# Batch 1's attention in four visits instead of six, and the first two w_in groups of batches 1 and 2 interleaved

## The chip, the cores and the metric

One core of one Trainium2 chip. The metric is the device time of one execution in microseconds (us).

## The reference, cut to what matters

```python
batch, n_heads, seq, head_dim = (8, 8, 1024, 64);  k_proj = 64
k_proj = np.einsum('ks,bhsd->bhkd', E, k)
v_proj = np.einsum('ks,bhsd->bhkd', F, v)
scores = scale * np.matmul(q, k_proj.transpose(0, 1, 3, 2))
attn = softmax(scores)                       # cut: max, exp, sum
attn_out = np.matmul(attn, v_proj)
x = attn_out.transpose(0, 2, 1, 3).reshape(8192, 512)
h = x @ w_in                                 # 512 -> 2048
g = h * np.clip(h + 3.0, 0.0, 6.0) / 6.0
return g @ w_out                             # 2048 -> 512
```

The two large products dominate. Attention is small, so the kernel hides it among them.

## The kernel before: the parts that the change and the argument touch

A batch has two blocks (t = 0, 1) of 512 tokens. A block has 16 `first_group`s (w_in, four matmuls each, one for each pair of heads in x, then ScalarE and VectorE make g) and four `second_group`s (w_out, 16 matmuls each). While they run, the attention of the next batch is computed in *visits*: TensorE leaves the w_out group for a round of small matmuls, 64 rows and columns each, four at a time in the array, and comes back. The program uses PSUM as two rings of four banks, `pmm` and `pat`.

Batch 1's attention has a plan of its own. It is spread over block 1 of batch 0, one `next(ahead)` for each four w_out matmuls:

```python
PLAN = ((0, "project"), (0, "keys_out"), (1, "turn"), (0, "values_out", 0), (2, "values_out", 1),
        (1, "two_scores", 0), (2, "two_scores", 2), (2, "normalised", 0),
        (0, "normalised", 1), (0, "normalised", 2), (0, "normalised", 3))
```

That makes six visits: two of `two_scores` (four banks of pat), four of `normalised` (two banks of sums, two of values). The later batches use larger visits, six banks each, of which the last one matters here:

```python
def visit(self, n, following, later):
    ...                                       # n = 0, 1, 2
    early = self.values(2, pmm, pmm)
    den, av = self.sums(3, pmm, pat), self.values(3, pat, pat)
    if following:
        following.project()                   # k and v of the batch after
    self.scaled(2, early, self.recs)          # VectorE: x of pair 2, both blocks
    recs = self.inverses(den)                 # ScalarE: Ln, Ln, Exp, Exp
    if following:
        following.keys_out()                  # VectorE: two copies of the keys
        later += [following.turn] + [lambda a=a: following.values_out(a) for a in range(2)]
    return lambda: self.scaled(3, av, recs)   # VectorE: x of pair 3, called next
```

For batch 2 this last visit is also the last thing before batch 2's own first block, which needs that x. In the later batches there is a whole block between.

The softmax here doesn't subtract the row's maximum and nothing guards it: scores larger than these inputs give would overflow.

## Time and profile before

| | before |
|---|---|
| median, lowest, highest of three runs | 511.65, 511.52, 511.9 us |
| span of the profiled run | 510.0 us |
| TensorE busy | 497.4 us, 98% |
| longest wait of TensorE after the first 48 us | 1.2 us, for x, at batch 2's start |

The prediction below shows the lines and reads them. In a line of a profile, PE is TensorE, PEld its weight loads, DVE VectorE, ACT ScalarE, POOL GpSimd and SPq the queue that issues DMAs. `at` and `mm` are banks of `pat` and `pmm`, `kp` and `kT` keys, `vp` values, `rec` the inverses of the sums, `o_sb` rows of the output. A bracket at the end of a timeline row gives the engine's idle time before the row, and what ended it.

### The profile page before, as it was taken

Reading aid. Unit: us, or ns where it says so; the run is one execution under the profiler, and the core shown is the slowest. Engines: PE = TensorE matmul, PEld = TensorE weight load, DVE = VectorE, ACT = ScalarE, POOL = GpSimd, SP = SyncE. Lnnn points to the kernel's source line nnn. Section 1 sums busy time; section 2 is a strip of 40 time slices with the busy share of each in tenths; the row PEclk is TensorE's granted clock in tenths of the full one; section 3 lists DMA queues with packets and bytes.
Section 4 is the critical chain, followed back from the end, with each engine's and each line's share of the span. In section 5 each row is a group of like instructions: output and inputs, shape, how many; then the busy total and the mean of one; then the engine's idle time right before and its main releaser. Section 6 shows DMA issues by size and latency. Waiting matters only on the chain.

```text
span 510.0 us, 7106 instructions
## 1 busy us (share of the span) xinstructions
PE 497.4 (98%) x2750; PEld 224.3 (44%) x2802; DVE 257.5 (50%) x401; ACT 274.5 (54%) x493; POOL 37.9 (7%) x57
## 2 busy tenths in 40 slices
PE   8899999999899999999999999999999999999996
PEld 3444444444344444444444444444444444444442
DVE  3572735855655733656434743467444563334420
ACT  3657476567576545664466644674447654444431
POOL 8610020010100200002000020000000000000000
PEclk9999999999999999999999999999999999999999
DMA  9999999599299493516924188421110111101112
GB/s 165 199 205 207 202 156 236 97 159 176 88 184 186 91 218 76 125 41 91 225 57 94 52 141 169 107 58 33 42 41 25 38 42 42 42 21 42 41 51 74
DMA packets 74210, 55.39 MB, mean 109 GB/s; under 512 B 35520, under 2 KB 65984, under 8 KB 74176
## 3 DMA queue, kind: packets, MB, share of 16 engines
q0 software_dynamic: 31952, 29.36, 37.0%
q1 hardware_dynamic: 42000, 25.17, 19.4%
q10 hardware_dynamic: 224, 0.39, 0.3%
q8 instruction: 22, 0.36, 0.3%
q14 instruction: 12, 0.10, 0.1%
HBM read 59.24 MB, written 16.78 MB: 149 GB/s over the span
## 4 chain that ended last, share of the span: by engine, by line
PE 94%; DMA 3%; issue 1%; POOL 1%; DVE 0%; ACT 0%; DVEq 0%; POOLq 0%
PE mm L470 43%; PE mm L450 43%; PE at L181 3%; DMA w_in_sb<-in_moe_w_in_dram 2%; PE at L227 1%; PE mm L227 1%; DMA k<-in_k_dram 1%; PE at L209 1%; PE mm L209 0%; PE at L370 0%; POOL q L97 0%; DVE kp L187 0%; POOL k L101 0%; PE at L350 0%; DVE xT L246 0%
## 5 line engine op out<-in xcount | busy, mean ns | idle before, releaser
L456 DVE SCALAR_TENSOR_TENSOR g<-r,mm 128x512 bf16<-128x512 f32 x256 | 173.8, 686 | 131.8 <-ACT r L455 130.4
L470 PE MATMUL mm<-w_out_sb,g 128*128 128x512 bf16 x995 | 231.8, 379 | 1.7 <-issue 0.5
L450 PE MATMUL mm<-xT,w_in_sb 128*128 128x512 bf16 x1001 | 229.2, 379 | 3.1 <-DVE xT L246 1.2
L455 ACT ACTIVATE r<-mm 128x512 f32<-128x512 f32 x256 | 152.8, 599 | 76.2 <-PE mm L450 73.7
L450 PEld LDWEIGHTS <-w_in_sb 128*128 128x128 bf16 x1024 | 99.4, 98 | 124.0 <-issue 5.5
L470 PEld LDWEIGHTS <-g 128*128 128x128 bf16 x1024 | 98.0, 98 | 121.5 <-issue 7.2
L484 ACT COPY o_sb<-mm 128x512 f32<-128x512 f32 x35 | 20.3, 587 | 91.5 <-PE mm L470 91.5
L484 DVE COPY o_sb<-mm 128x512 f32<-128x512 f32 x28 | 19.3, 691 | 67.3 <-PE mm L470 64.2
L159 ACT ACTIVATE rec<-mm 128x512 f32<-128x512 f32 x34 | 19.0, 595 | 34.1 <-PE mm L227 17.6
L163 ACT ACTIVATE rec<-rec 128x512 f32<-128x512 f32 x60 | 35.6, 637 | 0.0
L246 DVE TENSOR_TENSOR xT<-at,rec 128x512 bf16<-128x512 f32 x44 | 28.1, 680 | 7.1 <-ACT rec L163 7.1
L218 ACT ACTIVATE aT<-at 128x512 bf16<-128x512 f32 x44 | 23.1, 613 | 0.9 <-PE at L209 0.9
L159 ACT ACTIVATE rec<-at 128x512 f32<-128x512 f32 x30 | 17.3, 598 | 6.0 <-PE at L227 3.7
L199 POOL COPY mark<-kT 1x1 bf16<-1x1 bf16 x5 | 0.9, 178 | 210.1 <-DMA kT<-kp 210.1
L181 PE MATMUL at<-k,e_t 128*64 128x512 bf16 x56 | 13.4, 382 | 0.0
L181 PE MATMUL at<-v,f_t 128*64 128x512 bf16 x56 | 13.4, 382 | 0.0
L187 DVE CAST kp<-at 64x512 bf16<-64x512 f32 x14 | 9.0, 678 | 4.9 <-PE at L181 4.9
L218 ACT ACTIVATE aT<-mm 128x512 bf16<-128x512 f32 x12 | 6.5, 594 | 8.9 <-PE mm L209 8.9
L190 DVE CAST vp<-at 64x512 bf16<-64x512 f32 x14 | 9.7, 694 | 0.4
L181 PEld LDWEIGHTS <-e_t 128*64 128x64 bf16 x56 | 5.6, 109 | 7.2 <-PE at L227 2.1
L479 DVE COPY o_sb<-mm 128x256 f32<-128x256 f32 x1 | 0.4, 425 | 16.0 <-PE mm L470 16.0
L227 PE MATMUL at<-aT,vp 64*64 64x512 bf16 x88 | 8.5, 376 | 0.0
(62 smaller groups left out, 147.0 us busy)
## 6 DMA issues: line engine op xcount, KB each, us to landing
out_dram<-o_sb SPq DMA_DIRECT2D x63, 256.0 KB, 2.0
k<-in_k_dram POOLq DMA_DIRECT2D x7, 1024.0 KB, 15.4
v<-in_v_dram POOLq DMA_DIRECT2D x7, 1024.0 KB, 21.0
q<-in_q_dram POOLq DMA_DIRECT2D x7, 1024.0 KB, 10.5
w_out_sb<-in_moe_w_out_dram POOLq DMA_DIRECT2D x4, 512.0 KB, 17.1
k<-in_k_dram POOLq DMA_DIRECT2D x4, 256.0 KB, 5.8
v<-in_v_dram POOLq DMA_DIRECT2D x4, 256.0 KB, 7.9
w_in_sb<-in_moe_w_in_dram POOLq DMA_DIRECT2D x2, 512.0 KB, 11.9
```

Of the source, the lines that this page charges most:

```text
L159: nc.scalar.activation(ln, den, AF.Ln)
L163: nc.scalar.activation(ln, ln, AF.Exp, scale=-1.0)
L181: nc.tensor.matmul(ps[e * KP:(e + 1) * KP], ef_t[e][:, so, :], kqv[self.b]["kv"[e]][:, :, so, :], start=(so == 0), stop=(so == SO - 1))
L190: nc.vector.tensor_copy(self.vp[a * KP:(a + 1) * KP], self.ps[KP:].rearrange("p (h d) -> p h d", d=D))
L218: nc.scalar.activation(self.aT[j][:, r].rearrange("p a n -> p (a n)"), tiles[r], AF.Exp, scale=scale)
L227: nc.tensor.matmul(tiles[t][c:c + D].rearrange("p (r n) -> p r n", r=2), stationary(r, 2 * j + a), self.aT[j][r:r + KP, :, a, :], start=Tr ...
L246: nc.vector.tensor_mul(self.xT[:, j, t, :], av[t], recs[t])
L450: nc.tensor.matmul(h_ps, w_in_sb[:, ko, fo * P:(fo + 1) * P], xT[:, ko, t, :], start=(ko == 0), stop=(ko == KO - 1))
L455: nc.scalar.activation(r, h_ps, AF.Relu, bias=0.5, scale=1.0 / 6.0)
L456: nc.vector.scalar_tensor_tensor(g[:, fo, :], r, 1.0, h_ps, op0=ALU.min, op1=ALU.mult)
L470: nc.tensor.matmul(o_ps, g[:, fo, c * P:(c + 1) * P], w_out_sb[:, fo, :], start=(fo == 0), stop=(fo == FO - 1))
L484: (copy or nc.scalar.copy)(o_sb, o_ps)
```

## The change

Its intent: fewer visits, so that TensorE leaves its stream less often; and matmuls that don't need the late pair of x put ahead of the one that waits for it. `PLAN`, `steps`, `two_scores` and `normalised` go. The core of the rest:

```diff
-    for fo in range(2, FO):                      # block 1 of batch 0
-        if fo in (7, 8, 9, 10):
-            next(ahead)
+        pop()
+        if fo == 7:
+            second.project()
+            second.keys_out()
+            later += [second.turn, *(lambda a=a: second.values_out(a) for a in range(2))]
 ...
+    rest = []
     for c in range(SB):
-        for _ in second_group(0, 1, g[1], c, nc.vector.tensor_copy):
-            next(ahead, None)
+        for i, _ in enumerate(second_group(0, 1, g[1], c, nc.vector.tensor_copy)):
+            pop()
+            if i == 0:
+                rest.append(second.visit(c, None, later))
+            elif i == 2 or c == SB - 1:
+                while rest:
+                    rest.pop()()
 ...                                               # main loop, batch b, block t
-                first_group(xT, t, g, fo)
+                if b < 3 and t == 0 and fo < 2:
+                    if fo == 0:
+                        two_groups(xT, t, g, ((0, 1, 2), (3,)))
+                else:
+                    first_group(xT, t, g, fo)
```

`two_groups` with `((0, 1, 2), (3,))` runs pairs 0 to 2 of the first group, pairs 0 to 2 of the second, then pair 3 of each.

More of the change, by code (lines that the diff above doesn't have):

```diff
@@ L281, in visit @@
             return lambda: self.scaled(3, av, recs)
-        def two_scores(self, j):
-            tiles = [self.scores(i, pat) for i in (j, j + 1)]
-            for i in range(2):
-                self.exps(j + i, tiles[i])
-        def normalised(self, j):
-            den, av = self.sums(j, pat, pat), self.values(j, pat, pat)
-            recs = self.inverses(den)
-            yield
-            self.scaled(j, av, recs)
-            yield
-            yield
-        def steps(self, plan):
-            for wait, part, *args in plan:
-                for _ in range(wait):
-                    yield
-                yield from getattr(self, part)(*args) or ()
-    PLAN = ((0, "project"), (0, "keys_out"), (1, "turn"), (0, "values_out", 0), (2, "values_out", 1),
-            (1, "two_scores", 0), (2, "two_scores", 2), (2, "normalised", 0),
-            (0, "normalised", 1), (0, "normalised", 2), (0, "normalised", 3))
     class First:
@@ L503, with two_groups @@
     g = [g_tile(), g_tile()]
-    def two_groups(t, kos, more):
+    def two_groups(xT, t, g, kos, more=lambda: None):
         tiles = [pmm(), pmm()]
@@ L512, in two_groups @@
         for fo in range(2):
-            h_out(tiles[fo], g[t], fo)
-    two_groups(0, ((0, 1), (2,), (3,)), lambda: next(by_pairs, None))
+            h_out(tiles[fo], g, fo)
+    two_groups(xT, 0, g[0], ((0, 1), (2,), (3,)), lambda: next(by_pairs, None))
     for fo in range(2, FO):
@@ L519, with pop @@
             first.queries(1, (0, 1) if fo == FO - 2 else (2, 3))
-    ahead = Attention(1)
-    ahead.xT = x_next
-    ahead = ahead.steps(PLAN)
+    behind, later = [], []
+    second = Attention(1)
+    second.xT = x_next
+    def pop():
+        if later:
+            later.pop(0)()
     rows = [second_group(0, 0, g[0], c) for c in range(SB)]
@@ L530 @@
             first.second_values(2 * i - 2)
-    two_groups(1, ((0, 1), (2, 3)), lambda: None)
+    two_groups(xT, 1, g[1], ((0, 1), (2, 3)))
     for fo in range(2, FO):
         first_group(xT, 1, g[1], fo)
-        if fo in (7, 8, 9, 10):
-            next(ahead)
+        pop()
[3 more added lines that the diff above has]
+            later += [second.turn, *(lambda a=a: second.values_out(a) for a in range(2))]
         elif fo == 11:
             whole(rows[3])
+    rest = []
     for c in range(SB):
-        for _ in second_group(0, 1, g[1], c, nc.vector.tensor_copy):
-            next(ahead, None)
+        for i, _ in enumerate(second_group(0, 1, g[1], c, nc.vector.tensor_copy)):
[5 more added lines that the diff above has]
+                    rest.pop()()
     qT_dma[2] = q_transposed(2)
-    whole(ahead)
     xT = x_next
-    behind, later = [], []
     second = Attention(2)
@@ L558 @@
             for fo in range(FO):
-                first_group(xT, t, g, fo)
-                if later:
-                    later.pop(0)()
+                if b < 3 and t == 0 and fo < 2:
[3 more added lines that the diff above has]
+                    first_group(xT, t, g, fo)
+                pop()
                 if b > 1 and t == 0 and fo == 5 and third:
```

## The prediction

> **What bounds the kernel now.** I read the page first (who is busy), then the waits of TensorE, then the chain, then the timeline of the two places that the change touches.
>
> ```profile
> PE 497.4 (98%) x2750; PEld 224.3 (44%) x2802; DVE 257.5 (50%) x401; ACT 274.5 (54%) x493; POOL 37.9 (7%) x57
> ...
> PE 94%; DMA 3%; issue 1%; POOL 1%; DVE 0%; ACT 0%; DVEq 0%; POOLq 0%
> PE mm L470 43%; PE mm L450 43%; PE at L181 3%; DMA w_in_sb<-in_moe_w_in_dram 2%; PE at L227 1%; PE mm L227 1%; DMA k<-in_k_dram 1%; PE at L209 1%; PE mm L209 0%; PE at L370 0%; POOL q L97 0%; DVE kp L187 0%; POOL k L101 0%; PE at L350 0%; DVE xT L246 0%
> ```
>
> TensorE is busy for 98% of a span of 510.0 us and is 94% of the chain that ends last; no other engine is over 54%. The change adds and removes no matmul, so it can only take away time in which TensorE starts none. The waits of TensorE between 48 and 136 us, the stretch that the change touches, show one real wait:
>
> ```profile
> PE mm L450 <- DVE xT L246: 1.2, 1, 1.2
> ```
>
> The unit for the rest is the spacing of 512-column matmuls. The chain in order of time gives it, as two neighbouring pieces of 16:
>
> ```profile
> 171.94 3.45 PE mm L470 x16
> 175.40 3.45 PE mm L450 x16
> ```
>
> 3.45/16 = 0.216 us from start to start. (The 379 ns of one matmul in the page is pipelined; I don't add those.)
>
> First place: batch 1's attention, which block 1's w_out groups hide. TensorE's timeline (start, length, then what):
>
> ```profile
> 70.58 0.63 PE L209 MATMUL at<-qT,kT 64*64 64x256 bf16 x16
> 71.14 1.90 PE L470 MATMUL mm<-w_out_sb,g 128*128 128x512 bf16 x8
> 72.97 0.41 PE L227 MATMUL at<-aT,ones 64*64 64x512 bf16 x4
> ...
> 76.23 0.41 PE L227 MATMUL at<-aT,ones 64*64 64x512 bf16 x4
> 76.47 0.39 PE L227 MATMUL at<-aT,vp 64*64 64x512 bf16 x4
> 76.78 2.76 PE L470 MATMUL mm<-w_out_sb,g 128*128 128x512 bf16 x12
> 79.48 0.41 PE L227 MATMUL at<-aT,ones 64*64 64x512 bf16 x4
> ```
>
> Here are six visits to the attention: two of 16 score matmuls (68.19, 70.58) and four of 4 sums and 4 values (72.97, 76.23, 79.48, 82.73). From the 12 matmuls at 76.78 to the visit at 79.48 pass 2.70 us, where 12 x 0.216 = 2.59: about 0.1 lost on the way in. A visit itself takes 76.78 - 76.23 = 0.56 us to the next w_out matmul, for two rounds of four concurrent tiles, which at 0.216 each would be 0.43: the other 0.1 is the way out. The same kernel already has visits of six banks, in batch 1's own second block:
>
> ```profile
> 114.00 0.41 PE L227 MATMUL mm<-aT,ones 64*64 64x512 bf16 x4
> ...
> 114.24 0.39 PE L227 MATMUL at<-aT,vp 64*64 64x512 bf16 x4
> ...
> 114.45 0.39 PE L209 MATMUL at<-qT,kT 64*64 64x256 bf16 x8
> ...
> 114.77 1.41 PEld L470 LDWEIGHTS <-g 128*128 128x128 bf16 x8 [0.20 <-issue]
> ```
>
> Three rounds of four in 114.77 - 114.00 = 0.77 us.
>
> Second place: the start of batch 2's first block, where the one wait lies.
>
> ```profile
> 133.92 0.82 PE L450 MATMUL mm<-xT,w_in_sb 128*128 128x512 bf16 x2
> 134.05 1.28 DVE L187 CAST kp<-at 64x512 bf16<-64x512 f32 x2 [0.76 <-PE at L181]
> 135.26 1.27 DVE L246 TENSOR_TENSOR xT<-at,rec 128x512 bf16<-128x512 f32 x2
> 135.98 2.97 PE L450 MATMUL mm<-xT,w_in_sb 128*128 128x512 bf16 x13 [1.25 <-DVE xT L246]
> ```
>
> The first w_in group runs its pairs 0 to 2 (one of the three records is missing), then its fourth matmul waits for pair 3 of x, which VectorE writes only after two copies of the next batch's keys. The fourth could have started about 134.58 (133.92, 0.01 of switching, 3 x 0.216); it starts at 135.98: 1.40 us lost.
>
> **What the Trainium skill says.** "TensorEngine Tiling (Array Packing)", Key Properties: "Changing tiling mode (not just tile) drains the TensorE". The trace agrees: about 0.1 us each way. "TensorE: Matmul & The Clock Gate", Wait — 56ns, not 53.3ns?, gives 215.7 ns from start to start for 512 columns at full clock; the trace has 216. The same page, Architectural detail, says that ScalarE and VectorE queues are strict first in, first out; so x behind the key copies is what the DVE lines above show. "Perfetto Trace Analysis", Matmuls, asks that independent groups rotate through different PSUM banks so that evacuation overlaps; that is the condition that the larger visits must meet.
>
> **The change part by part.**
>
> (a) Six visits become four of six banks. Removed: six ways in of 0.10 and six visits of 0.56 us, 0.60 + 3.36 = 3.96. Added: four ways in of 0.10 and four visits of 0.77, 0.40 + 3.08 = 3.48. Saved: 0.48 us, all on TensorE's own stream, so all on the path, if no visit has to wait. Finer sums of the single starts give 0.46.
>
> The visits now come after the first four matmuls of each of four w_out groups, so every 16 x 0.216 + 0.10 + 0.77 = 4.33 us, against 7.8 us where the kernel has such visits already. Who must keep up? Visit 0 starts where the first score visit did, 68.19; queries and keys landed before 67.06 (the GpSimd copy that waits for them). Visit 1, at 72.52, needs exponentials: ScalarE takes six at 0.52 from 68.64, done 71.8, the pair needed by sums at 70.7. Visit 2, at 76.85, needs the banks of pair 0's values: in the old visit at 72.97 the second product ends at 76.34, 3.37 later, so now at 75.9. Visit 3, at 81.18, needs the inverses of pair 2: ScalarE after visit 2 has four Ln at 0.54 and four Exp at 0.58, 4.5 us from 77.3, done 81.8; only VectorE waits for the last of them. It multiplies pair 2 until about 83.1, and pair 3 (Ln and Exp after visit 3, first done about 83.5) until 84.9. Batch 1's first block then starts at about 84.56 instead of 85.03, and needs pair 3 half a microsecond or more later: no wait. The banks: in the compiled program of the kernel before, 384 of 392 tiles of the ring of four take the bank that was released longest ago in program order. By that order no visit takes the bank of the w_out group just ended, except visit 3's denominators, which take the bank of the group that ended 1.4 us before; its copy needs 0.43 + 0.69 = 1.12 us.
>
> (b) Batch 2's first two groups: three matmuls of the second group go ahead of the wait. The wait's end is set by VectorE (keys, then x), which this does not move against the visit. So 3 x 0.216 = 0.65 us of the 1.40 is filled, and 0.75 stays. After it both groups end within 0.43 us, and VectorE falls behind: products at about 137.0 and 137.7, a value copy, the third product until about 139.9. The next visit would come at 139.96 (140.61 less 0.65) and wants that bank: it just fits, or loses 0.1.
>
> (c) The same at batch 1's start saves nothing: the chain shows no wait there before, and by (a) none after. Value copies one group later, no more and no fewer instructions elsewhere.
>
> Sum: -0.46 - 0.65 = -1.11 us; 511.65 - 1.11 = 510.54. With a tenth lost to the tight places I say 510.6, a gain of 0.2%.
>
> **The rivals.** First: bank waits in the closer visits. If the first w_in group of batch 1 or a visit's tile gets the bank of a w_out group that has just ended, TensorE stands 1.12 - 0.22 = 0.9 us each time (copy latency less one spacing), and (a) turns to a loss: 511.5 with one, 514 with four. For it: visits 4.33 us apart and VectorE copies behind products in one queue. Against: the order of release above. Second: ScalarE or VectorE becomes the bound in this stretch: ScalarE was busy 12.9 of the 17.8 us from 67.2 to 85.0, the same work now fits in 17.3, 75%; for it, the work bunches; against it, nothing is needed sooner than a visit later. It would cost some tenths: 511.0. Third: the filled 0.65 us is given back at batch 2's next visit, whose banks and keys (landed by 138.15) then bind: 511.2. Fourth: the filled wait is worth nothing because x comes later; I see no reason in the DVE order.
>
> **Range and chances.** The three runs before lie within 0.4 us. All rivals but four-fold bank waits stay between 510.4 and 511.7. I give 510.2 to 511.4. A 2% change would need 10 us, ten times what TensorE idles in these places.
>
> **What would show it right or wrong.** Right: four visits of about 0.77 us in block 1, 4.33 us apart; batch 1's first w_in matmul near 84.6; the wait for x at batch 2 present still, at about 0.6 in the list of waits instead of 1.2, with six w_in matmuls ahead of it; later pieces of the chain all shifted by about 1.1 us. Wrong: a new wait of TensorE on an o_sb copy, on rec or on g in 68 to 90 us, or on g at batch 2's first visit; or x of pair 3 later than 2.05 us after the first w_in matmul of batch 2.

## The result, and the profile after

Six runs: 510.52 us median (510.4 to 510.6), against 511.5 us (511.27 to 511.9) for six runs of before: 0.98 us less. The ratio of the two is 0.998, 95% interval 0.9967 to 0.9993. It is a small gain, clear of the noise, and "the same" by a 2% measure.

(Line numbers differ between the profiles, since the change removes lines: w_in is L450 before and L424 after, w_out L470 and L444.) The page has TensorE as busy as before in a shorter span (508.7 us):

```profile
PE 497.5 (98%) x2750; PEld 224.3 (44%) x2802; DVE 258.0 (51%) x401; ACT 274.0 (54%) x493; POOL 37.9 (7%) x57
```

TensorE's timeline in block 1 (start, length, line, what):

```profile
68.11 0.61 PE L209 MATMUL at<-qT,kT 64*64 64x256 bf16 x16
68.65 3.63 PE L444 MATMUL mm<-w_out_sb,g 128*128 128x512 bf16 x16
72.21 0.41 PE L227 MATMUL mm<-aT,ones 64*64 64x512 bf16 x4
...
76.54 0.41 PE L227 MATMUL mm<-aT,ones 64*64 64x512 bf16 x4
76.78 0.39 PE L227 MATMUL at<-aT,vp 64*64 64x512 bf16 x4
77.00 0.39 PE L227 MATMUL at<-aT,ones 64*64 64x512 bf16 x4
77.31 3.63 PE L444 MATMUL mm<-w_out_sb,g 128*128 128x512 bf16 x16
80.87 0.41 PE L227 MATMUL mm<-aT,vp 64*64 64x512 bf16 x4
```

Visits start 4.33 us apart (72.21, 76.54, 80.87), and the one at 76.54 takes 77.31 - 76.54 = 0.77 us. No row of the whole stretch has a wait for a bank.

The start of batch 2's first block, all engines:

```profile
133.14 1.47 PE L424 MATMUL mm<-xT,w_in_sb 128*128 128x512 bf16 x5
133.28 1.28 DVE L187 CAST kp<-at 64x512 bf16<-64x512 f32 x2 [0.76 <-PE at L181]
134.48 1.27 DVE L246 TENSOR_TENSOR xT<-at,rec 128x512 bf16<-128x512 f32 x2
...
135.21 2.32 PE L424 MATMUL mm<-xT,w_in_sb 128*128 128x512 bf16 x10 [0.60 <-DVE xT L246]
...
139.01 0.69 DVE L190 CAST vp<-at 64x512 bf16<-64x512 f32 x1
...
139.43 0.74 PE L209 MATMUL at<-qT,kT 64*64 64x256 bf16 x16
```

Six matmuls run before the wait (five recorded; a few per cent of the records are missing), where three ran before. The wait, marked 1.25 before, is 0.60 now. And something new: the last rounds of scores of batch 2's first visit take 0.74. The same row of the kernel before has 0.61:

```profile
140.85 0.61 PE L209 MATMUL at<-qT,kT 64*64 64x256 bf16 x16
```

To place the difference I took single starts of TensorE from both traces and cut the run into stretches. The wait in this table is the distance between the two w_in starts less one spacing of 0.216, so a little more than the profile's own figure.

| stretch (us) | before | after | difference |
|---|---|---|---|
| start to the key projection of batch 1 | 55.009 | 54.689 | -0.320 |
| from there to batch 1's first w_in matmul (block 1) | 30.017 | 29.556 | -0.461 |
| from there to batch 2's first w_in matmul | 48.891 | 48.893 | +0.002 |
| from there to the end of batch 2's first visit | 7.471 | 6.964 | -0.507 |
| of it: the wait for x | 1.408 | 0.764 | -0.644 |
| of it: the visit | 0.782 | 0.919 | +0.137 |
| from there to the end | 368.647 | 368.646 | -0.001 |

The stretches are from one profile of each kernel. The two that the change touches give -0.461 - 0.507 = -0.968 us, and the medians say -0.98. The -0.320 of the first stretch is no part of it: nothing is changed there, and over the twelve profiles that stretch lasts 54.39 to 55.01 us, with the profile of before at the top.

### The profile page after: what moved, and what is told of

Read it like the earlier page. It is cut to its first block, busy times and chain, and to the rows that moved or that the text cites. A ratio compares the mean times of both kernels' runs of the same rounds, so it can differ in the third digit from the quotient of the medians. Undisturbed runs are those within 1.5% of the kernel's fastest.

```text
span 508.7 us, 7106 instructions
## 1 busy us (share of the span) xinstructions
PE 497.5 (98%) x2750; PEld 224.3 (44%) x2802; DVE 258.0 (51%) x401; ACT 274.0 (54%) x493; POOL 37.9 (7%) x57
## 4 chain that ended last, share of the span: by engine, by line
PE 94%; DMA 2%; POOL 2%; issue 1%; DVE 0%; ACT 0%; DVEq 0%; POOLq 0%
PE mm L444 44%; PE mm L424 43%; PE at L181 3%; DMA v<-in_v_dram 2%; PE mm L227 2%; PE at L227 1%; PE at L209 1%; POOL q L97 1%; PE mm L209 1%; POOL k L101 1%; POOL v L101 0%; PE at L344 0%; DVE kp L187 0%; PE at L324 0%; PE at L312 0%
## 5 line engine op out<-in xcount | busy, mean ns | idle before, releaser
L444 PE MATMUL mm<-w_out_sb,g 128*128 128x512 bf16 x997 | 231.6, 379 | 1.8 <-issue 0.6
L424 PE MATMUL mm<-xT,w_in_sb 128*128 128x512 bf16 x999 | 229.1, 379 | 1.8 <-DVE xT L246 0.6
L424 PEld LDWEIGHTS <-w_in_sb 128*128 128x128 bf16 x1024 | 99.4, 98 | 122.8 <-issue 4.8
L444 PEld LDWEIGHTS <-g 128*128 128x128 bf16 x1024 | 98.1, 98 | 121.6 <-issue 7.0
L159 ACT ACTIVATE rec<-mm 128x512 f32<-128x512 f32 x39 | 21.8, 595 | 37.0 <-PE mm L227 20.1
L246 DVE TENSOR_TENSOR xT<-at,rec 128x512 bf16<-128x512 f32 x42 | 26.9, 680 | 5.1 <-ACT rec L163 5.1
L159 ACT ACTIVATE rec<-at 128x512 f32<-128x512 f32 x25 | 14.6, 599 | 2.3 <-PE at L344 2.3
L218 ACT ACTIVATE aT<-mm 128x512 bf16<-128x512 f32 x14 | 7.6, 594 | 9.5 <-PE mm L209 9.5
L246 DVE TENSOR_TENSOR xT<-mm,rec 128x512 bf16<-128x512 f32 x14 | 9.0, 682 | 0.6 <-PE mm L227 0.6
L84 PE MATMUL mm<-ones 128*128 128x512 bf16 x18 | 7.4, 548 | 1.5 <-DVE ones L77 1.5
```

The costliest lines, as they stand in the source:

```text
L159: nc.scalar.activation(ln, den, AF.Ln)
L218: nc.scalar.activation(self.aT[j][:, r].rearrange("p a n -> p (a n)"), tiles[r], AF.Exp, scale=scale)
L246: nc.vector.tensor_mul(self.xT[:, j, t, :], av[t], recs[t])
L424: nc.tensor.matmul(h_ps, w_in_sb[:, ko, fo * P:(fo + 1) * P], xT[:, ko, t, :], start=(ko == 0), stop=(ko == KO - 1))
L444: nc.tensor.matmul(o_ps, g[:, fo, c * P:(c + 1) * P], w_out_sb[:, fo, :], start=(fo == 0), stop=(fo == FO - 1))
```

## The experiments

Ten runs in three calls, the first on chip 9, the others on chip 13. Each is set beside runs of before on its own chip. Differences of some tenths in the medians are near the spread of the runs, since the start varies: by the runs' times alone, visits alone (95% interval of the ratio to before 0.9977 to 1.0002) and five visits (0.9973 to 1.0) are not clear of the noise. The stretches after the start repeat to 5 ns where an edit leaves them alone, the long last one to 0.03 us, so the verdicts rest on them.

| kernel | median (us) | before, same chip | block 1 stretch | wait for x, batch 2 | batch 2's first visit |
|---|---|---|---|---|---|
| visits alone | 511.01 | 511.44 | 29.556 | 1.410 | 0.781 |
| pair alone | 510.90 | 511.44 | 30.018 | 0.762 | 0.919 |
| no pair at batch 1 | 510.70 | 511.44 | 29.556 | 0.763 | 0.918 |
| x first | 509.72 | 511.44 | 29.555 | 0 | 0.919 |
| five visits | 510.72 | 511.38 | 29.787 | 0.763 | 0.919 |
| late visit | 510.26 | 511.38 | 29.556 | 0.763 | 0.782 |
| x first, late visit | 509.60 | 511.38 | 29.556 | 0 | 0.782 |
| after again | 510.42 | 511.46 | 29.556 | 0.762 | 0.918 |
| x first, no pair | 509.53 | 511.46 | 29.556 | 0 | 0.782 |
| value copy on ScalarE | 510.36 | 511.46 | 29.555 | 0.764 | 0.782 |

### One part at a time

`visits_alone` is the changed kernel without the interleaved groups:

```diff
-                if b < 3 and t == 0 and fo < 2: ... two_groups ...   # cut
-                else:
-                    first_group(xT, t, g, fo)
+                first_group(xT, t, g, fo)
```

> Batch 1's attention in four visits, batches 1 and 2 start as before. My theory (a tiling switch costs 0.1 us each way, nothing else in block 1): block 1's w_out stretch is 0.46 us shorter than before, the wait for x at batch 2 is the whole 1.41 us again, no loss in batch 2's first visit; about 0.46 us under before, 0.5 over the changed kernel. Rival (the two parts help each other, or the visits shift later waits): something clearly else than 0.46.

`pair_alone` is the kernel before (six visits) with the interleaved groups at batch 2 only (cut: `two_groups` takes `xT` and `g`, as in the change):

```diff
-                first_group(xT, t, g, fo)
+                if b == 2 and t == 0 and fo < 2:
+                    if fo == 0:
+                        two_groups(xT, t, g, ((0, 1, 2), (3,)))
+                else:
+                    first_group(xT, t, g, fo)
```

> The old six visits, and the paired start only at batch 2. My theory: 0.65 us of the wait filled, 0.14 given back in batch 2's first visit, where the score tiles wait for the bank of the value copy; 0.51 us under before, and the two parts alone add up to the whole 0.97. Rival (the filled time is given back entirely, or the end of the wait moves): 0 to 0.2 under before.

Measured: the visits alone shorten block 1 by 0.461 us and leave the wait at 1.41; the pair alone shortens the wait by 0.646 and lengthens the visit by 0.137, and leaves block 1 as it was. In the medians that is 0.43 and 0.54 us; together 0.97, what the whole change gives. The parts are independent, and the longer visit belongs to the pair.

`no_pair_batch1` keeps all but the interleaving at batch 1 (`b < 3` becomes `b == 2`).

> The changed kernel, but batch 1's first two groups not interleaved. My theory: the x of batch 1 is there before its first group asks for it, so the pair there does nothing: equal to the changed kernel within 0.05 us in the trace. Rival (with visits closer together, pair 3 of batch 1 comes late and the pair hides it): a new wait for x near 85 us, up to 0.65 us slower.

Measured: the stretches of the table as in the changed kernel to 3 ns, no wait at batch 1. The "batch 1" half of that edit does nothing, because its x is there in time either way. (The median is 0.2 us above the changed kernel's, which ran on another chip. Its profile's start is 0.2 us longer, 54.895 us, and the rest agrees to 0.02 us.)

### Is it the number of visits?

`five_visits` cuts visit 1 of block 1 in two, so that its score round comes four w_out matmuls later:

```diff
             if n == 1:
                 den, av = self.sums(0, pmm, pmm), self.values(0, pat, pat)
-                last = self.scores(3, pat)
                 recs = self.inverses(den)
-                self.exps(3, last)
+                if self.b > 1:
+                    self.exps(3, self.scores(3, pat))
 ...
+            elif i == 1 and c == 1:
+                second.exps(3, second.scores(3, pat))
```

> The changed kernel with visit 1 of block 1 cut in two: its eight score matmuls come four w_out matmuls later as a fifth visit. My theory (each visit costs two tiling switches and nothing else): from the first key projection to batch 1's first w_in matmul 29.56 us in the changed kernel, here 29.78 (0.10 in, 0.1 out, 0.01 each of two rounds that start cold); 0.2 us slower in the trace. Rival (the gain came from where visits lie against the banks, not from their number): no difference, or far more than 0.2.

TensorE's timeline of that kernel, around the added visit:

```profile
71.95 0.41 PE L227 MATMUL mm<-aT,ones 64*64 64x512 bf16 x4
72.19 0.39 PE L227 MATMUL at<-aT,vp 64*64 64x512 bf16 x4
72.51 1.04 PE L444 MATMUL mm<-w_out_sb,g 128*128 128x512 bf16 x4
73.48 0.41 PE L209 MATMUL at<-qT,kT 64*64 64x256 bf16 x8
73.82 2.76 PE L444 MATMUL mm<-w_out_sb,g 128*128 128x512 bf16 x12
```

The four w_out matmuls from 72.51 to the visit at 73.48 take 0.97 us where a full stream takes 0.86: the way in, plus 0.01 of a slower first start. The score round takes 73.82 - 73.48 = 0.34 us. The stretch is 29.787 us, 0.231 longer than with four visits. One visit more costs 0.23, two fewer gave 0.461: the price is per visit, and the rival (it is where they lie against the banks) falls.

The loss comes with the change of tile shape, not whenever TensorE turns to another product. In the profile of before, after the first 21.5 us, 30 of 33 starts of a round of 64x64 tiles came 0.309 or 0.310 us after the 128x128 matmul before them. From w_in to w_out, both 128x128, it was 0.215 or 0.216 in 51 of 54. (The others, at 0.525 and 0.43, are one spacing longer: a record is missing.) What fills the 0.093 us stays open. At a change, the weight load starts with its matmul (both at 139.18 in the changed kernel, in batch 2's first visit), where in a stream it starts about 0.2 us ahead (63.56 and 63.78 in the kernel before). So a late weight load and a drained array would look alike here, and no run separates them.

### What sets the end of the wait?

`x_first` splits the product for pair 3. The half that batch 2's first block needs goes ahead of the key copies in VectorE's queue:

```diff
             if following:
+                nc.vector.tensor_mul(self.xT[:, 3, 0, :], av[0], recs[0])
                 following.keys_out()
                 later += [following.turn] + [...]
+                return lambda: nc.vector.tensor_mul(self.xT[:, 3, 1, :], av[1], recs[1])
             return lambda: self.scaled(3, av, recs)
```

> The changed kernel, with VectorE's product for pair 3 of the first half of x ahead of the two key copies (the other half stays behind them). My theory (the wait is set by VectorE's order, not by ScalarE's inverses or by TensorE): the first inverse is done about 0.6 us before the key copies start, so the wait at batch 2 of 0.76 us is gone; key copies start about 0.15 us later and nobody waits for them; 0.76 us under the changed kernel, less if batch 2's first visit then waits longer. Rival (x is late because its inverses are late): at most 0.2 us better.

Measured: the wait is gone, and from batch 2's first w_in matmul to the end of its first visit it is 6.203 us against 6.964, 0.761 less. So x was late only because two copies that nobody waited for yet stood ahead of it.

`x_first_no_pair` is the same without any interleaved groups:

> Four visits, the first half of pair 3's product ahead of the key copies, and no group interleaved at the start of batches 1 and 2. My theory (VectorE's order alone makes the wait): x is there about 0.3 us before the fourth matmul of batch 2 asks for it, so there is no wait with or without the pair; and as the two groups no longer end together, VectorE is not behind in the next visit, which takes 0.78 us again instead of 0.92. 0.14 us under the kernel with x first and the pair; 0.9 under the changed kernel. Rival (the pair is still needed): a wait for x of 0.2 to 0.6 us at batch 2.

All engines of that kernel at batch 2's start:

```profile
132.67 0.69 DVE L279 TENSOR_TENSOR xT<-at,rec 128x512 bf16<-128x512 f32 x1 [0.30 <-ACT rec L163]
...
133.00 3.63 PE L426 MATMUL mm<-xT,w_in_sb 128*128 128x512 bf16 x16
133.28 1.27 DVE L187 CAST kp<-at 64x512 bf16<-64x512 f32 x2
```

The product ends at 132.67 + 0.69 = 133.36; the fourth matmul is due three spacings and 0.01 after 133.00, at 133.66. The 16 records of w_in matmuls run in one piece, without a wait. The visit is back at 0.782. This version beats both kernels: 509.53 us, 1.93 under before and 0.89 under the changed kernel on the same chip.

`after_again` was run for that comparison.

> The changed kernel once more, on the chip of the two runs below, so that their medians can be held against it: about 1.0 us under before; the stretches of its trace equal to the first to a few ns, the first 48 us different by some tenths.

It gave 510.42 us, 1.04 under before, with the stretches of the first profile.

### What made batch 2's first visit longer?

`late_visit` makes that one visit after twelve w_out matmuls instead of eight:

```diff
                     next(rows)
                     next(rows)
+                    if b == 2 and n == 0:
+                        next(rows)
                     rest = second.visit(n, third, later)
```

> The changed kernel, with batch 2's first visit after twelve instead of eight matmuls of its w_out group. My theory (the 0.14 us lost in that visit is the wait of its last score tile for the bank that the second value copy still reads): the visit takes 0.78 us again instead of 0.92, nothing else moves; 0.14 us better in the trace. Rival (the visit is longer for another reason, such as ScalarE being behind): still 0.92.

Measured: 0.782. A visit that comes 0.86 us later has nothing to wait for. But that does not say which bank it was. `value_copy_scalar` moves only the second value copy for batch 3, which reads the bank of its projection, to ScalarE:

```diff
         def values_out(self, a):
-            nc.vector.tensor_copy(self.vp[a * KP:(a + 1) * KP], self.ps[KP:]...)
+            copy = nc.scalar.copy if self.b == 3 and a == 1 else nc.vector.tensor_copy
+            copy(self.vp[a * KP:(a + 1) * KP], self.ps[KP:]...)
```

> The changed kernel, with the second value copy of batch 3's projection on ScalarE instead of VectorE, so that its bank is free some 1.8 us sooner; the visit stays where it is. My theory (the last score tile waits for that bank, not for a product on VectorE): batch 2's first visit takes 0.78 us instead of 0.92, so 0.14 us in the trace. Rival (it waits for the third product's bank, as I predicted): VectorE's third product is not moved, and the visit still takes 0.92.

All engines of that kernel:

```profile
138.28 0.69 DVE L431 SCALAR_TENSOR_TENSOR g<-r,mm 128x512 bf16<-128x512 f32 x1
138.28 0.58 ACT L191 CAST vp<-at 64x512 bf16<-64x512 f32 x1 [1.00 <-DVE vp L191]
...
139.41 0.61 PE L210 MATMUL at<-qT,kT 64*64 64x256 bf16 x16
```

The third product on VectorE still starts at 138.28 (138.29 in the changed kernel), and the rounds take 0.61 again, the visit 0.782. In the changed kernel the value copy ended at 139.01 + 0.69 = 139.70, and the last score tile, due at 139.65, started at 139.76 (single starts from its trace; the start waits for a semaphore that VectorE raises). So the visit waited for the value copy's bank. My expectation had a flaw of its own: the bank came free 0.84 us sooner (138.86), not 1.8, as ScalarE's copy waited for VectorE's copy of the other half (the row's bracket). That was enough.

`x_first_late` puts both repairs into the changed kernel:

> Both repairs: the first half of pair 3's product ahead of the key copies, and batch 2's first visit after twelve matmuls. My theory: both are independent, 0.76 + 0.14 = 0.90 us under the changed kernel from batch 2's start to the end, 1.9 us under before in all, about 509.6. Rival: the keys, copied later, now hold up the visit and part of it is lost.

Measured: 509.60 us, no wait, the visit at 0.782. From batch 2's start to the end of the visit, with the four moved matmuls (0.863) taken off, 6.065 us against 6.964: 0.90, as expected. Leaving the pair out (6.066) gives the same with less code.

## Why the prediction was right

510.6 us were predicted, from a sum of 510.54; the result is 510.52.

- **(a) Six visits to four.** Predicted 0.46 to 0.48, measured 0.461. Visits came 4.33 us apart and took 0.77, as predicted. Batch 1's first w_in matmul was due near 84.6 and came at 84.25; 0.32 of that is the earlier start. `five_visits` confirms the cost of a visit, 0.23.
- **(b) The pair at batch 2.** Predicted 0.65 filled and 0.75 left; measured 0.644 and 0.764. `x_first` shows that VectorE's order sets the end of the wait, as the chain of reasons said.
- **The tenth given back.** The prediction had the next visit "just fit, or lose 0.1", and put that to the third product's bank. It lost 0.137, but to the bank of the second value copy, which comes right after that product in VectorE's queue. The size was about right, the bank wrong: the prediction looked only at the mm ring for that visit, not at the at ring.
- **(c) The pair at batch 1 saves nothing.** Shown by `no_pair_batch1`.
- **The rivals.** No bank wait in block 1 and no delay from ScalarE or VectorE there: the stretch is shorter by the whole 0.461. (The count that the prediction held against bank waits, 384 of 392 tiles, is of the compiled program; no trace or run here shows it.) Of the third rival 0.14 of 0.65 us came true. The fourth (x later) did not: x came 2.069 us after batch 2's first w_in matmul, 2.067 before. The limit of 2.05 that the prediction gave for this was itself set too low; the profile before already exceeded it.
- **The size of it all.** The medians the prediction started from were three runs at 511.65. With six they were 511.5, so part of the exact hit is luck: the difference was predicted as 1.1 and measured as 0.98.

## What to carry to other kernels

Before you fill a wait with other work, look at what stands ahead of the awaited instruction in its engine's queue: here one product moved ahead of two copies removed the whole 1.4 us, where interleaving filled 0.65 and cost 0.14 again, because two groups that end together leave the evacuating engine behind. When small matmuls of another tiling interrupt a stream, count the interruptions, and check every bank ring that a visit draws from. And judge a change of 0.2% by stretches of the trace between the same instructions, not by whole times alone.

## What the Trainium skill lacked or had wrong

- "TensorEngine Tiling (Array Packing)", Key Properties, says that a change of tiling mode drains TensorE, but no cost. Here a change of tile shape cost 0.093 us on the way in (0.309 from start to start instead of 0.216) and about the same on the way out (0.308); a whole added visit cost 0.231 us besides its matmuls. That the time goes to a drain is the page's word; no run here separates it from the weight load.
- "TensorE: Matmul & The Clock Gate", Back-to-back issue gap, gives about 131 ns for each 512-column matmul in a stream of weight loads and matmuls. Streams of such pairs here ran at 216 ns (16 in 3.45 us), at a granted clock of 1.00; of 1956 spacings in the profile of before, none is under 215 ns. The 215.7 ns of the same page's other section fits.
